# Chunk attention and a Mish feed-forward on one core: transposes behind the output products, one inversion of the sums for two tiles

## The chip, the core and the metric

The kernel runs on one core of a Trainium2 chip. A core has TensorE (products into PSUM), VectorE, ScalarE, GpSimd and SyncE (which here issues the DMAs). Each engine works through its own queue in order and waits at semaphores for the others. The metric is the time of one execution on the device in microseconds (us); a profiled execution also leaves a trace with the start and length of every instruction.

## The reference

Attention within chunks of 64 tokens, for 8 sequences of 576 tokens and 8 heads of 64; then a feed-forward with w_in 512 x 2048 and w_out 2048 x 512 over all 4,608 tokens:

```python
scores = scale * np.matmul(q_c, k_c.transpose(0, 1, 2, 4, 3))
scores = scores - np.max(scores, axis=-1, keepdims=True)
attn = np.exp(scores)
attn = attn / (np.sum(attn, axis=-1, keepdims=True) + 1e-09)
out = np.matmul(attn, v_c)
...
h = x @ w_in
sp = np.where(h > 20.0, h, np.log1p(np.exp(np.minimum(h, 20.0))))
g = h * np.tanh(sp)
return (g @ w_out).astype(np.float32)
```

## The kernel before

**Tiles.** A tile is 128 tokens, two chunks. A *pair* is two tiles (256 tokens), a *block* is two pairs (512 tokens), and there are 9 blocks, 18 pairs. Everything that needs precision goes through TensorE as two fp32r parts, a high one and the rest (`xh`, `xl` for the attention's result, `wi_h`, `wi_l`, `wo_h`, `wo_l` for the weights, `gh`, `gl` for the gate).

**Slots.** The main loop has a slot for each step `s` = 0 to 144, one for each of 16 groups of 128 columns of w_in in each block, and one more to finish. In slot `s` TensorE runs `up(s + 1)`, twelve products of 512 columns into the PSUM tile `h` (of which two exist), and `down(s - 1)`, twelve products into the four accumulators `o`. ScalarE turns `h` into `z` by `mish(s + 1)`; VectorE (in every second step of the first block ScalarE) makes `gh` of it in `g_hi(s)`, and VectorE `gl` in `g_lo(s)`. `down(s - 1)` needs `gh` and `gl` of the slot before.

**The weights.** They come as 64-bit numbers and are taken apart during the first 16 slots, two of them in each slot: ScalarE scales (`w_scale`, two instructions), VectorE puts the bits together (`w_bits`, two), ScalarE rounds to the high part (`w_hi`), VectorE subtracts (`w_lo`). In slot `s` this ends with `wo` of column group `s`, which `down(s)` needs in the next slot, and `wi` of group `s + 3`. The tile between the two engines (`wic`, `woc`, tag `c`) has three buffers: a scaling needs the one that VectorE's subtraction, three weights earlier, gives back.

**The attention of a pair** is spread over seven slots `k0` to `k0 + 6` by `plan`: scores (0), max and subtraction (1), Exp, sum, inversion (2), norm (3), transposes and their copy to SBUF (4), values products (5), the two parts of x (6). `k0` is 1 and 8 in the first block, and 16 more for each block on, so the transposes of the first two steady pairs stand in slots 5 and 12. The scores `s`, the transposes `pt` and the values products `av` all use one PSUM tile, tag `a` (`HOME`), of which there is one: each must have been read out before the next is written. The values products need both the copy `ps` and that tile.

**The order** on each engine is the order in which the code is written (`manual_schedule`), so the calls in `slot` set it. In slot 4 of a pair TensorE has `up`, transposes, `down`; ScalarE has the high part of one weight, in even slots `gh`, two scalings, the copy, `mish`, the high part of the next weight, two scalings.

**The prologue** does pairs 0 and 1 tile by tile (`FIRST`, `SECOND`), the two tiles in different PSUM tiles, with the weights' first steps in between. `keep_busy(n)` puts `n` filler products (two records each in the trace) into TensorE's queue ahead of a wait; they write to a tile nobody reads.

Of the kernel before, what the change touches and what calls it, by code (L numbers as in the profile page):

```python
# [9 lines left out]
F32 = mybir.dt.float32  # L10
# [4 lines left out]
ALU = mybir.AluOpType  # L15
AX = mybir.AxisListType

P = 128
CHUNK = 64
# [4 lines left out]
def kernel(  # L24
# [17 lines left out]
    nc = tc.nc  # L42
# [7 lines left out]
    NG = H // 2  # L50
# [4 lines left out]
    sm_p = ctx.enter_context(tc.tile_pool(name="sm", bufs=2))  # L55
# [74 lines left out]
    def w(step, n):  # L130
        if n < len(order):
            steps[step](*order[n])


    st = {}
    xts = {}
    BOTH = slice(0, 2)
# [44 lines left out]
    def small(j, name, t):  # L182
        n = t.stop - t.start
        o = sm_p.tile([P, 2, n * NG], F32, name=f"{name}_{j}_{t.start}", tag=name)
        st[j][name, t.start] = o
        return o
# [21 lines left out]
    def a_exp(j, t=BOTH):  # L208
        p = st[j]["p"][:, t]
        nc.scalar.activation(out=p, in_=p, func=AF.Exp, scale=SCALE)  # L210

    def a_inverse(j, t=BOTH):
        p = st[j]["p"][:, t].rearrange("p t g c k -> p (t g) c k")
        r = small(j, "r", t)
        nc.vector.tensor_reduce(out=r.rearrange("p c n -> p n c"), in_=p, op=ALU.add, axis=AX.X)  # L215
        nc.vector.tensor_scalar(out=r, in0=r, scalar1=1e-9, scalar2=None, op0=ALU.add)
        nc.vector.reciprocal(out=r, in_=r)

    def a_norm(j, t=BOTH):
        p = st[j]["p"][:, t].rearrange("p t g c k -> p c (t g) k")  # L220
        r = st[j]["r", t.start]
        nc.vector.tensor_tensor(  # L222
            out=p, in0=p, in1=r.unsqueeze(3).broadcast_to([P, 2, r.shape[2], CHUNK]), op=ALU.mult
        )

    def a_transpose(j, ts=BOTH, place=HOME):
        d = st[j]
        d["pt", ts.start] = place[0].tile([P, 2, NG, P], F32, name=f"pt_{j}_{ts.start}", tag=place[1])
        for t in range(ts.start, ts.stop):
            for g in range(NG):  # L230
                nc.tensor.transpose(  # L231
                    out=d["pt", ts.start][:, t - ts.start, g],
                    in_=d["p"][:, t, g].rearrange("p c k -> p (c k)"),
                    identity=ident,
                )

    def a_copy(j, t=BOTH):
        d = st[j]
        if t.start == 0:
            d["ps"] = at.tile([P, 2, H, CHUNK], F32, name=f"ps_{j}", tag="A")  # L240
        nc.scalar.copy(  # L241
            out=d["ps"][:, t].rearrange("p t h k -> p (t h k)"),
            in_=d["pt", t.start][:, : t.stop - t.start].rearrange("p t g n -> p (t g n)"),
        )

    def a_values(j, t=BOTH, place=HOME):
        small_mm(banks(j, "av", t, place), st[j]["v"], st[j]["ps"], t)
# [110 lines left out]
    FIRST, SECOND = slice(0, 1), slice(1, 2)  # L358

    def prologue():  # L360

        A, B = slice(0, PTOK), slice(PTOK, TOK)
        O0, O2 = (ps_o, "o0"), (ps_o, "o2")
        room = xp.tile([P, 2, 2, H, CHUNK], F32, name="room_qk", tag="xh")
        room_v = xp.tile([P, 2, 2, H, CHUNK], F32, name="room_v", tag="xl")
        load_qk(0, None, (FIRST, SECOND), (nc.sync, nc.scalar))
        w("load", 0)
        load_v(0, room_v[:, 0])
        load_qk(1, (room[:, 0], room[:, 1]), (FIRST, SECOND))
        w("load", 1)  # L370
        load_v(1, room_v[:, 1])
        w("load", 2)
        w("load", 3)
        for t, place in (FIRST, HOME), (SECOND, O0):
            keep_busy(7 if t == FIRST else 3)
            a_scores(0, t, place)
            a_max(0, t)
            a_sub(0, t)
            a_exp(0, t)
        w("scale", 0)  # L380
        for t, place in (FIRST, O2), (SECOND, HOME):
            a_inverse(0, t)
            a_norm(0, t)
            keep_busy(9 if t == FIRST else 3)
            a_transpose(0, t, place)
            a_copy(0, t)
        w("bits", 0)
        w("hi", 0)
        w("lo", 0)
        for t, place in (FIRST, O0), (SECOND, O2):  # L390
            a_values(0, t, place)
        for t in FIRST, SECOND:
            a_hi(0, t)
            a_lo(0, t)
        w("scale", 1)
        for t, place in (FIRST, HOME), (SECOND, O0):
            a_scores(1, t, place)
            a_max(1, t)
            a_sub(1, t)
            a_exp(1, t)  # L400
        w("scale", 2)
        w("load", 4)
        up(0, A)
        for t, place in (FIRST, O2), (SECOND, HOME):
            a_inverse(1, t)
            a_norm(1, t)
            keep_busy(8 if t == FIRST else 4)
            a_transpose(1, t, place)
            a_copy(1, t)
        w("bits", 1)  # L410
        w("hi", 1)
        w("bits", 2)
        for t, place in (FIRST, O0), (SECOND, O2):
            a_values(1, t, place)
        for t in FIRST, SECOND:
            a_hi(1, t)
            a_lo(1, t)
        w("hi", 2)
        w("scale", 3)
        w("load", 5)  # L420
        w("lo", 1)
        w("lo", 2)
        w("bits", 3)
        w("scale", 4)
        up(0, B)
        up(1, last="w")
        mish(0)
        load_qk(2)
        w("load", 6)
# [8 lines left out]
    def slot(s):  # L438
        a = plan.get(s, {})
        n = 2 * s + 3  # L440

        if 1 <= s and s + 1 < N:
            up(s + 1, last="w")
        if 4 in a:
            a_transpose(a[4])
        if 5 in a:
            a_values(a[5])
        if 0 in a:
            a_scores(a[0])
        if 1 <= s <= N:  # L450
            down(s - 1)

        w("load", n + 4)
        w("hi", n)
        if s < N:
            g_hi(s)
            g_lo(s)
        w("scale", n + 2)
        w("bits", n + 1)
        w("lo", n)  # L460
        if 1 in a:
            a_max(a[1])
        if 3 in a:
            a_norm(a[3])
        if 4 in a:
            a_copy(a[4])
        if 2 in a:
            a_exp(a[2])

        w("load", n + 5)  # L470
        if 6 in a:
            a_hi(a[6])
        if s + 1 < N:
            mish(s + 1)
        w("hi", n + 1)
        w("scale", n + 3)
        w("bits", n + 2)
        w("lo", n + 1)
        if 1 in a:
            a_sub(a[1])  # L480
        if 2 in a:
            a_inverse(a[2])
        if 6 in a:
            a_lo(a[6])
        if -2 in a and a[-2] > 2:
            load_qk(a[-2])
        if 1 in a:
            load_v(a[1])
        if s >= 1 and s % NF == 0:
            store(s // NF - 1)  # L490
# [43 lines left out]
```

## Time and profile before

| | |
|---|---|
| median of 3 runs | 878.25 us (878.2 to 879.17) |
| the profiled execution | 878.64 us, its span 876.9 us |
| TensorE busy | 860.9 us (98%), 5984 instructions |
| weight loads of TensorE | 709.4 us (81%) |
| VectorE busy | 342.9 us (39%), 534 instructions |
| ScalarE busy | 253.4 us (29%), 360 instructions |
| mean granted clock of TensorE | 0.996 |

The profile has a page with sums over the span, and the trace answers questions on stretches, engines and single instructions. A row of the trace in order of time gives the start in us, the length, the engine, the line of the kernel, the operation, output and inputs, and how many like instructions in a row it stands for; in brackets the idle time of the engine ahead of it and what ended that. L162 is a score or values product, L201 the subtraction of the maximum, L210 Exp, L215 to L217 sum, addition and reciprocal, L222 the norm, L231 a transpose, L241 the copy, L288 `up`, L300 `mish`, L308 and L313 `gh` and `gl` on VectorE, L326 `down`, L356 a filler, L89 and L93 the two scalings, L99 the bits, L114 and L117 the high and the low part of a weight. The products of TensorE overlap: the start of the next is the surer measure, the end of one is modelled. The granted clock is a share of full speed: 1.00 is 2.4 GHz and 0.50 is 1.2 GHz.

### The profile page before, as it was taken

Reading aid. Unit: us, or ns where it says so; the run is one execution under the profiler, and the core shown is the slowest. Engines: PE = TensorE matmul, PEld = TensorE weight load, DVE = VectorE, ACT = ScalarE, POOL = GpSimd, SP = SyncE. Lnnn points to the kernel's source line nnn. Section 1 sums busy time; section 2 is a strip of 40 time slices with the busy share of each in tenths; the row PEclk is TensorE's granted clock in tenths of the full one; section 3 lists DMA queues with packets and bytes.
Section 4 is the critical chain, followed back from the end, with each engine's and each line's share of the span. In section 5 each row is a group of like instructions: output and inputs, shape, how many; then the busy total and the mean of one; then the engine's idle time right before and its main releaser. Section 6 shows DMA issues by size and latency. Waiting matters only on the chain.

```text
span 876.9 us, 13659 instructions
## 1 busy us (share of the span) xinstructions
PE 860.9 (98%) x5984; PEld 709.4 (81%) x5984; DVE 342.9 (39%) x534; ACT 253.4 (29%) x360; POOL 0.7 (0%) x6
## 2 busy tenths in 40 slices
PE   7989999999999999999999999999999999999996
PEld 7778888888888888888888888888888888888885
DVE  6898844242434233323424242423242243322221
ACT  4887832121312122221213131212222131321111
POOL 0000000000000000000000000000000000000000
PEclk9999999999999999999999999999999999999999
DMA  6657612101310120111120121012011201001002
GB/s 265 218 183 227 191 40 58 49 25 49 73 49 25 49 73 25 50 28 53 41 73 4 46 73 49 25 50 73 35 39 49 63 24 59 1 5 44 1 0 49
DMA packets 25180, 55.41 MB, mean 63 GB/s; under 512 B 2592, under 2 KB 2592, under 8 KB 25120
## 3 DMA queue, kind: packets, MB, share of 16 engines
q1 hardware_dynamic: 24832, 54.01, 20.6%
q8 instruction: 47, 0.77, 0.4%
q10 hardware_dynamic: 288, 0.52, 0.2%
q14 instruction: 13, 0.11, 0.0%
HBM read 45.09 MB, written 9.44 MB: 62 GB/s over the span
## 4 chain that ended last, share of the span: by engine, by line
PE 91%; DVE 5%; ACT 3%; issue 1%; DMA 0%; SPq 0%; POOLq 0%; POOL 0%; DVEq 0%; ACTq 0%
PE o L326 43%; PE h L288 41%; PE s L162 2%; PE av L162 2%; PE pt L231 2%; DVE wic L99 1%; DVE woc L99 1%; DVE p L222 1%; PE spare L356 0%; DVE m L189 0%; DVE wo_l L117 0%; ACT L300 0%; DVE r L215 0%; DVE wi_l L117 0%; ACT L210 0%
## 5 line engine op out<-in xcount | busy, mean ns | idle before, releaser
L308 DVE CAST gh<-z 128x512 fp32r<-128x512 f32 x136 | 57.9, 426 | 455.9 <-PE o L326 455.9
L326 PE MATMUL o<-wo_h,gl 128*128 128x512 f32 x576 | 229.6, 399 | 0.0
L326 PE MATMUL o<-wo_l,gh 128*128 128x512 f32 x576 | 225.2, 391 | 0.1
L326 PE MATMUL o<-wo_h,gh 128*128 128x512 f32 x576 | 225.3, 391 | 0.0
L300 ACT ACTIVATE z<-h 128x512 f32<-128x512 f32 x144 | 86.1, 598 | 454.3 <-PE h L288 348.5
L288 PE MATMUL h<-xh,wi_l 128*128 128x512 f32 (+1 forms) x580 | 154.4, 388 | 0.9 <-ACT xh L262 0.9
L288 PE MATMUL h<-xl,wi_h 128*128 128x512 f32 (+1 forms) x580 | 154.2, 388 | 0.3 <-ACT z L300 0.3
L288 PE MATMUL h<-xh,wi_h 128*128 128x512 f32 (+1 forms) x580 | 154.2, 388 | 0.0
L326 PEld LDWEIGHTS o<-wo_h,gl 128*128 128x128 f32 x576 | 108.5, 188 | 23.3
L288 PEld LDWEIGHTS h<-xh,wi_l 128*128 128x128 f32 x580 | 108.4, 188 | 23.4 <-ACT xh L262 1.0
L326 PEld LDWEIGHTS o<-wo_h,gh 128*128 128x128 f32 x576 | 108.5, 188 | 22.8
L288 PEld LDWEIGHTS h<-xl,wi_h 128*128 128x128 f32 x580 | 108.2, 188 | 22.9 <-ACT z L300 0.7
L288 PEld LDWEIGHTS h<-xh,wi_h 128*128 128x128 f32 x580 | 108.4, 188 | 22.3
L326 PEld LDWEIGHTS o<-wo_l,gh 128*128 128x128 f32 x576 | 108.6, 189 | 21.8 <-DVE wo_l L117 0.5
L313 DVE TENSOR_TENSOR gl<-z,gh 128x512 fp32r<-128x512 f32 x144 | 99.6, 692 | 9.5 <-ACT gh L306 4.8
L241 ACT COPY ps<-pt 128x1024 f32<-128x1024 f32 (+1 forms) x20 | 18.6, 928 | 83.4 <-PE pt L231 83.4
L338 DVE COPY ob<-o 128x512 f32<-128x512 f32 x18 | 12.5, 692 | 52.7 <-ACT ob L340 30.9
L300 ACT ACT_TABLE_LOAD x17 | 21.8, 1283 | 34.5 <-PE h L288 34.5
L231 PE MATMUL pt<-ident,p 128*128 128x128 f32 x144 | 19.1, 273 | 5.6 <-DVE p L222 5.6
L189 DVE TENSOR_REDUCE m<-s 128x16 f32<-128x1024 f32 (+1 forms) x20 | 22.2, 1112 | 5.9 <-PE s L162 5.8
L231 PEld LDWEIGHTS pt<-ident,p 128*128 128x128 f32 x144 | 16.4, 139 | 8.8 <-issue 3.5
L162 PEld LDWEIGHTS s<-k,q 64*64 64x64 f32 x1088 | 17.9, 137 | 6.0 <-issue 5.9
(38 smaller groups left out, 384.5 us busy)
## 6 DMA issues: line engine op xcount, KB each, us to landing
out<-ob SPq DMA_DIRECT2D x72, 128.0 KB, 2.4
wis<-in_w_in SPq DMA_DIRECT2D x16, 512.0 KB, 3.6
wos<-in_w_out SPq DMA_DIRECT2D x16, 512.0 KB, 3.9
q<-in_q SPq DMA_DIRECT2D x16, 512.0 KB, 3.7
k<-in_k SPq DMA_DIRECT2D x16, 512.0 KB, 3.7
v<-in_v SPq DMA_DIRECT2D x16, 512.0 KB, 3.9
room_v<-in_v SPq DMA_DIRECT2D x2, 512.0 KB, 7.5
k<-in_k ACTq DMA_DIRECT2D x2, 256.0 KB, 3.9
```

The costliest lines, as they stand in the source:

```text
L99: nc.vector.scalar_tensor_tensor(out=c, in0=x, scalar=mask, in1=d["a"][:, :, 0] if op == ALU.logical_shift_left else c, op0=op, op1=ALU.bi ...
L162: nc.tensor.matmul(o[h * CHUNK : (h + 1) * CHUNK, c, t - ts.start, g], lhsT=l[rows, t, 2 * g + h], rhs=r[rows, t, 2 * g + h], start=True, ...
L189: nc.vector.tensor_reduce(out=small(j, "m", t), in_=st[j]["s", t.start].rearrange("p c t g k -> p c (t g) k"), op=ALU.max, axis=AX.X,)
L222: nc.vector.tensor_tensor(out=p, in0=p, in1=r.unsqueeze(3).broadcast_to([P, 2, r.shape[2], CHUNK]), op=ALU.mult)
L231: nc.tensor.transpose(out=d["pt", ts.start][:, t - ts.start, g], in_=d["p"][:, t, g].rearrange("p c k -> p (c k)"), identity=ident,)
L241: nc.scalar.copy(out=d["ps"][:, t].rearrange("p t h k -> p (t h k)"), in_=d["pt", t.start][:, : t.stop - t.start].rearrange("p t g n -> p ...
L288: nc.tensor.matmul(h[:, cols], lhsT=w_[:, f, kt], rhs=x[:, kt, cols], start=(n == 0), stop=(n == 3 * NK - 1),)
L300: nc.scalar.activation(out=d["z"], in_=d["h"], func=AF.Mish)
L308: nc.vector.tensor_copy(out=d["gh"], in_=d["z"])
L313: nc.vector.tensor_tensor(out=d["gl"], in0=d["z"], in1=d["gh"].bitcast(F32), op=ALU.subtract)
L326: nc.tensor.matmul(acc[t], lhsT=g[:, sl], rhs=w_[:, f], start=(f == 0 and n == 0), stop=(f == NF - 1 and n == 2),)
L338: nc.vector.tensor_copy(out=o, in_=acc[t])
```

## The change

In a slot, a pair's transposes move from between `up` and the output products to behind the output products, and their copy moves from the middle of that slot to the beginning of ScalarE's queue in the next one, ahead of the values products. The sum of a tile (`a_sum`) is separated from the addition and the reciprocal (`a_inverse`), which in the prologue now run once for both tiles of a pair, after both sums; the tile `r` is one for both, in the order tile, head group, chunk, and sum and norm run through `p` in its memory's order. Of the prologue the diff shows pair 0; pair 1 is changed alike.

```diff
-    def a_inverse(j, t=BOTH):
-        p = st[j]["p"][:, t].rearrange("p t g c k -> p (t g) c k")
-        r = small(j, "r", t)
-        nc.vector.tensor_reduce(out=r.rearrange("p c n -> p n c"), in_=p, op=ALU.add, axis=AX.X)
+    def a_sum(j, t=BOTH):
+        d = st[j]
+        if t.start == 0:
+            d["r"] = sm_p.tile([P, 2, 2 * NG], F32, name=f"r_{j}", tag="r")
+        nc.vector.tensor_reduce(
+            out=d["r"][:, t].rearrange("p t n -> p (t n)"),
+            in_=d["p"][:, t].rearrange("p t g c k -> p (t g c) k"),
...
+    def a_inverse(j):
+        r = st[j]["r"]
         nc.vector.tensor_scalar(out=r, in0=r, scalar1=1e-9, scalar2=None, op0=ALU.add)
         nc.vector.reciprocal(out=r, in_=r)
 
     def a_norm(j, t=BOTH):
-        p = st[j]["p"][:, t].rearrange("p t g c k -> p c (t g) k")
-        r = st[j]["r", t.start]
+        p = st[j]["p"][:, t].rearrange("p t g c k -> p (t g c) k")
+        r = st[j]["r"][:, t].rearrange("p t n -> p (t n)")
...
+        for t in FIRST, SECOND:
+            a_sum(0, t)
+        a_inverse(0)
         w("scale", 0)
         for t, place in (FIRST, O2), (SECOND, HOME):
-            a_inverse(0, t)
             a_norm(0, t)
             keep_busy(9 if t == FIRST else 3)
             a_transpose(0, t, place)
...
-        if 4 in a:
-            a_transpose(a[4])
         if 5 in a:
+            a_copy(a[5])
             a_values(a[5])
         if 0 in a:
             a_scores(a[0])
         if 1 <= s <= N:
             down(s - 1)
+        if 4 in a:
+            a_transpose(a[4])
...
-        if 4 in a:
-            a_copy(a[4])
...
         if 2 in a:
+            a_sum(a[2])
             a_inverse(a[2])
```

TensorE in slot 5 of the main loop (`h` is `up`, `o` is `down`, `pt` the transposes of pair 2), before:

```order
L288 MATMUL h_706<-xl_246,wi_h 128x512 x4
L288 MATMUL h_706<-xh_245,wi_h 128x512 x4
L288 MATMUL h_706<-xh_245,wi_l 128x512 x4
L231 MATMUL pt_0_719<-ident,p_598 128x128 x8
L326 MATMUL o_0_509<-wo_h,gl_686 128x512
L326 MATMUL o_0_509<-wo_l,gh_684 128x512
L326 MATMUL o_0_509<-wo_h,gh_684 128x512
```

And now, at the end of slot 5 and the beginning of slot 6:

```order
L335 MATMUL o_2_510<-wo_h,gl_680 128x512
L335 MATMUL o_2_510<-wo_l,gh_678 128x512
L335 MATMUL o_2_510<-wo_h,gh_678 128x512
L240 MATMUL pt_0_725<-ident,p_592 128x128 x8
L297 MATMUL h_758<-xl_243,wi_h 128x512 x4
L297 MATMUL h_758<-xh_242,wi_h 128x512 x4
L297 MATMUL h_758<-xh_242,wi_l 128x512 x4
```

The twelve output products, which stood behind the transposes, now stand ahead of them.

ScalarE in slots 5 and 6 (`ps` is the copy, `z` the gate activation, `wi_h` and `wo_h` the high parts of weights, `wic`, `wis` and `woc`, `wos` the scalings), before:

```order
L93 ACTIVATE wos_681<-wos_681 128x512
L241 COPY ps_753<-pt_0_719 128x1024
L300 ACTIVATE z_757<-h_706 128x512
L114 CAST wi_h<-wic_700 128x512
L89 ACTIVATE wic_760<-wis_695 128x512
L93 ACTIVATE wis_695<-wis_695 128x512
L114 CAST wo_h<-woc_747 128x512
L306 CAST gh_827<-z_757 128x512
```

And now:

```order
L93 ACTIVATE wos_681<-wos_681 128x512
L309 ACTIVATE z_749<-h_700 128x512
L114 CAST wi_h<-wic_694 128x512
L89 ACTIVATE wic_752<-wis_689 128x512
L93 ACTIVATE wis_689<-wis_689 128x512
L250 COPY ps_771<-pt_0_725 128x1024
L114 CAST wo_h<-woc_741 128x512
L315 CAST gh_821<-z_749 128x512
```

The copy moved behind the gate activation, a cast and two scalings; the two casts behind it are the first work of slot 6.

VectorE in the prologue, pair 0, from the second tile's maximum on (`m` maximum, `p` probabilities, `r` sums), before:

```order
L189 TENSOR_REDUCE m_1_165<-s_1_148 128x8
L201 TENSOR_TENSOR p_142<-s_1_148,m_1_165 128x2x4x64
L215 TENSOR_REDUCE r_0_172<-p_142 128x4x2
L216 TENSOR_SCALAR r_0_172<-r_0_172 128x8
L217 RECIPROCAL r_0_172<-r_0_172 128x8
L222 TENSOR_TENSOR p_142<-p_142,r_0_172 128x2x4x64
L215 TENSOR_REDUCE r_1_193<-p_142 128x4x2
L216 TENSOR_SCALAR r_1_193<-r_1_193 128x8
L217 RECIPROCAL r_1_193<-r_1_193 128x8
L222 TENSOR_TENSOR p_142<-p_142,r_1_193 128x2x4x64
```

And now:

```order
L189 TENSOR_REDUCE m_1_165<-s_1_148 128x8
L201 TENSOR_TENSOR p_142<-s_1_148,m_1_165 128x2x4x64
L216 TENSOR_REDUCE r_169<-p_142 128x8 x2
L225 TENSOR_SCALAR r_169<-r_169 128x16
L226 RECIPROCAL r_169<-r_169 128x16
L231 TENSOR_TENSOR p_142<-p_142,r_169 128x512 x2
```

Both sums now stand ahead of the first norm, and one addition and one reciprocal are gone. TensorE's order in the prologue, fillers included, is as before.

## Rows read from the trace of the kernel before

**Rows 1.** The page: an engine's busy time, and VectorE's largest group with its wait

```profile
PE 860.9 (98%) x5984; PEld 709.4 (81%) x5984; DVE 342.9 (39%) x534; ACT 253.4 (29%) x360; POOL 0.7 (0%) x6
...
L308 DVE CAST gh<-z 128x512 fp32r<-128x512 f32 x136 | 57.9, 426 | 455.9 <-PE o L326 455.9
```

**Rows 2.** Stretches: length, busy us of PE, PEld, DVE, ACT, POOL, clock, DMA

```profile
40.00:60.00 20.00, 17.45 (x81) 14.00 (x80) 18.46 (x28) 16.77 (x26) 0.00 (x0) 1.00 0.61 204
```

**Rows 3.** TensorE in order of time, slots 5 and 6

```profile
55.49 1.07 PE L288 MATMUL h<-xh,wi_l 128*128 128x512 f32 x4
59.03 1.06 PE L231 MATMUL pt<-ident,p 128*128 128x128 f32 x8 [2.46 <-DVE p L222]
...
67.11 1.16 PE L162 MATMUL av<-ps,v 64*64 64x64 f32 x64
```

**Rows 4.** Stretches in the prologue and in slot 5 (the clock is third from last)

```profile
11.00:12.00 1.00, 0.94 (x9) 0.75 (x7) 0.90 (x4) 0.58 (x1) 0.00 (x0) 1.00 0.93 365
...
60.50:61.00 0.50, 0.50 (x3) 0.38 (x2) 0.50 (x2) 0.50 (x2) 0.00 (x0) 0.50 0.00 0
```

**Rows 5.** Chain that ended last, merged: start, us, what; slot 5, then later slots

```profile
60.09 4.34 PE o L326 x12
...
152.66 2.72 PE h L288 x12
155.38 0.87 PE pt L231 x8
```

**Rows 6.** VectorE in order of time, slots 4 and 5, then slot 9

```profile
57.06 0.68 DVE L117 TENSOR_TENSOR wo_l<-woc,wo_h 128x512 fp32r<-128x512 f32 x1
57.67 1.22 DVE L222 TENSOR_TENSOR p<-p,r 128x1024 f32<-128x1024 f32 x1
...
63.12 0.69 DVE L117 TENSOR_TENSOR wo_l<-woc,wo_h 128x512 fp32r<-128x512 f32 x1
...
83.46 0.43 DVE L308 CAST gh<-z 128x512 fp32r<-128x512 f32 x1 [1.50 <-PE o L326]
```

**Rows 7.** ScalarE in order of time, slot 5

```profile
62.03 0.99 ACT L241 COPY ps<-pt 128x1024 f32<-128x1024 f32 x1
...
64.50 0.68 ACT L93 ACTIVATE wis<-wis 128x512 int32<-128x512 uint32 x1
```

**Rows 8.** All engines in order of time, slots 12 and 13

```profile
102.68 1.06 PE L231 MATMUL pt<-ident,p 128*128 128x128 f32 x8 [0.22 <-DVE p L222]
...
106.40 0.69 DVE L99 SCALAR_TENSOR_TENSOR wic<-wis,wic 128x512 uint32<-128x512 uint32 x1
...
107.47 0.61 ACT L114 CAST wi_h<-wic 128x512 fp32r<-128x512 f32 x1
...
109.11 0.61 ACT L114 CAST wo_h<-woc 128x512 fp32r<-128x512 f32 x1
...
109.15 1.16 PE L162 MATMUL av<-ps,v 64*64 64x64 f32 x64
```

**Rows 9.** All engines in order of time, the prologue's pair 0

```profile
8.77 0.63 ACT L210 ACTIVATE p<-p 128x512 f32<-128x512 f32 x1 [0.85 <-DVE p L201]
...
9.81 0.69 DVE L222 TENSOR_TENSOR p<-p,r 128x512 f32<-128x512 f32 x1
...
10.64 0.63 PE L231 MATMUL pt<-ident,p 128*128 128x128 f32 x4 [1.19 <-DVE p L222]
...
11.11 0.83 PE L356 MATMUL spare<-ident 128*128 128x128 f32 x6
...
12.41 0.63 PE L231 MATMUL pt<-ident,p 128*128 128x128 f32 x4 [0.47 <-DVE p L222]
```

**Rows 10.** Groups by form: busy us, mean ns of one, idle time before

```profile
L215 DVE TENSOR_REDUCE r<-p 128x8 f32<-128x512 f32 x4 | 2.7, 680 | 0.0
...
L217 DVE RECIPROCAL r<-r 128x16 f32<-128x16 f32 x16 | 4.1, 254 | 0.6
L216 DVE TENSOR_SCALAR r<-r 128x16 f32<-128x16 f32 x16 | 2.8, 175 | 0.5
```

More of the change, by code (lines that the diff above doesn't have):

```diff
@@ L210, in a_exp @@
         nc.scalar.activation(out=p, in_=p, func=AF.Exp, scale=SCALE)
-    def a_inverse(j, t=BOTH):
-        p = st[j]["p"][:, t].rearrange("p t g c k -> p (t g) c k")
-        r = small(j, "r", t)
-        nc.vector.tensor_reduce(out=r.rearrange("p c n -> p n c"), in_=p, op=ALU.add, axis=AX.X)
+    def a_sum(j, t=BOTH):
[5 more added lines that the diff above has]
+            in_=d["p"][:, t].rearrange("p t g c k -> p (t g c) k"),
+            op=ALU.add,
+            axis=AX.X,
+        )
+    def a_inverse(j):
+        r = st[j]["r"]
         nc.vector.tensor_scalar(out=r, in0=r, scalar1=1e-9, scalar2=None, op0=ALU.add)
@@ L219, in a_norm @@
     def a_norm(j, t=BOTH):
-        p = st[j]["p"][:, t].rearrange("p t g c k -> p c (t g) k")
-        r = st[j]["r", t.start]
+        p = st[j]["p"][:, t].rearrange("p t g c k -> p (t g c) k")
+        r = st[j]["r"][:, t].rearrange("p t n -> p (t n)")
         nc.vector.tensor_tensor(
-            out=p, in0=p, in1=r.unsqueeze(3).broadcast_to([P, 2, r.shape[2], CHUNK]), op=ALU.mult
+            out=p, in0=p, in1=r.unsqueeze(2).broadcast_to([P, r.shape[1], CHUNK]), op=ALU.mult
         )
@@ L400, in prologue @@
             a_exp(1, t)
+        for t in FIRST, SECOND:
+            a_sum(1, t)
+        a_inverse(1)
         w("scale", 2)
@@ L404, in prologue @@
         for t, place in (FIRST, O2), (SECOND, HOME):
-            a_inverse(1, t)
             a_norm(1, t)
```

## The prediction

> **What bounds the kernel now.** I read the page's busy shares first, then the stretches, then the order of time on single engines. TensorE is busy 98% of the span, and the largest group of VectorE has waited 455.9 us for TensorE's output products [rows 1]. So nearly everywhere TensorE is the bound, and moving work on the other two engines buys nothing there. The exception is the start: between 40 and 60 us TensorE is busy 17.45 of 20 us, VectorE 18.46 and ScalarE 16.77 [rows 2]. There the two engines split the weights into two parts, and TensorE runs into them. The largest hole is in slot 5, at the first steady pair's transposes: the last four products of `up` start at 55.49, one product takes 2.72 / 12 = 0.227 us [rows 3, 5], so what follows could start at 56.40; the transposes start at 59.03, because `p` is normalised from 57.67 to 58.89 [rows 3, 6]. A second cost follows: after TensorE stood 2.46 us, the granted clock is 0.50 at 60.5 us, that is 1.2 instead of 2.4 GHz [rows 3, 4], and the twelve output products there take 4.34 us against 2.72 for twelve elsewhere, 1.6 us more [rows 5]. What the change does to this stretch, to the same place of the next pair (slots 12 and 13) and to the prologue decides the time.
>
> **The slots in which TensorE is the bound (14 of 16 pairs).** Eight transposes cost 0.87 us between two blocks of products [rows 5]; moved from behind `up` to behind `down` they are as many, between the same two kinds of neighbours. The copy now starts when they end, while the next `up` (2.72 us) runs; it takes 0.99 [rows 7], so 1.7 us of cover is left before the values products need it. Without that cover each pair would pay up to 0.99. I take 0. No row shows transposes between `down` and `up`; the nearest others are the prologue's, four in 11.11 - 10.64 = 0.47 [rows 9], 0.94 for eight, 0.07 more than here. So I bound the move by 0.07 a pair either way, 1.0 us in all, for the range. The sum and the norm run through as many elements in another order, on an engine that waits: 0.
>
> **Slots 5 and 6 (the first steady pair).** All times here are on the clock of the profile before. In slot 5 the output products now stand right behind `up`. The first can start at 56.40. The second reads `wo_l`, which VectorE writes from 57.06 for 0.68 us [rows 6], so a new wait of about 1.2 us takes the place of the old one: the second starts near 57.8, the remaining eleven end near 60.4, the transposes (whose `p` is ready at 58.89) near 61.3, and `up` of slot 6 near 64.0. Up to here 3 us are won against before, where the values products started at 67.11 [rows 3].
> But these need the copy. In ScalarE's queue it now stands behind the rest of slot 5 (the gate activation, a cast, two scalings) and not ahead of them. The first of these scalings needs a buffer that VectorE gives back when it ends the row of 63.12, at 63.81 [rows 6]; so the two cannot move up, and the second stays at 64.50 [rows 7]. The copy follows near 65.1 and ends near 66.1. The values products start at 66.1 instead of 64.1, a wait of 2.0 us, and **the gain left is 67.1 - 66.1 = 1.0 us**. Queued behind the copy are the cast of `wo_h` and the cast of `gh`, for which VectorE's `gl` waits: VectorE comes up to 0.8 us late in slot 6. At 83.46 it stood 1.50 us waiting for TensorE [rows 6], which is where its delay and TensorE's lead meet; from there on all engines run about 1.0 us earlier.
>
> **Slots 12 and 13 (the second pair).** Before, the transposes waited 0.22 us by the row [rows 8], some 0.4 against the pitch; the move saves that. But the copy again moves behind the rest of its slot. The cast that stood at 107.47 needs bits that VectorE ends at 106.40 + 0.69 = 107.09, so it can start at 107.1. From that cast to the next slot's first ScalarE instruction it was 109.11 - 107.47 = 1.64 us [rows 8]. With the copy in that place it starts near 108.8, ends near 109.8, and the values products follow at 109.9 instead of 109.15 [rows 8]: **0.8 us lost**, the saved 0.4 included. The bounds: a gain of 0.4, if ScalarE were free in time, and a loss of 1.0, the whole copy.
>
> **The prologue (two pairs, where VectorE is on the path).** Before, the first tile's sum, addition, reciprocal and norm ran while the second tile was still in Exp. Now the second sum stands ahead of the first norm. Exp of the second tile ends at 8.77 + 0.63 = 9.40 [rows 9]; then come the sum 0.680, the addition 0.175, the reciprocal 0.254 [rows 10] with four hand-overs of some 0.04: the first norm starts near 10.65 instead of 9.81. One addition and one reciprocal fewer bring the second norm's end some 0.3 us forward. But on TensorE the fillers (`keep_busy`) stand between the two tiles' transposes. Before, the first transposes started 0.83 after their norm, at 10.64, the fillers at 11.11, and the second tile's transposes at 12.41, when their norm was there [rows 9]. Now the first start at 11.48, the fillers (six records, 0.11 from start to start as for the transposes) at 11.95, and the second tile's cannot start before 12.6: 0.2 late, although their norm is ready near 12.0. The second pair repeats the pattern with eight records: 0.84 + 0.47 + 0.88 = 2.19 against 12.41 - 10.64 = 1.77, 0.4 late. Of these 0.6 ScalarE's weight cast, which stands ahead of the next step, hides some 0.1: **0.5 us lost**, with 0.2 and 0.6 as bounds. Without the fillers it would be a gain of 0.3 a pair.
>
> **The sum.** -1.0 + 0.8 + 0.5 = +0.3 us. The profiled execution took 878.64 (876.9 of span and 1.74 around it), so 878.9; the median of the runs is 0.39 below that execution, hence **878.6**.
>
> **A rule weighed.** A wait of TensorE of 1.19 us left the granted clock at 1.00 [rows 4, 9], that of 2.46 us did not [rows 3, 4]; the new ones of 2.0 us lie between. [...]
>
> **The rivals.**
> *The clock falls again* (slower). Place: the 2.0 us wait ahead of the values products in slot 6. Price: 1.6 [rows 5]. It decides from where, between 1.19 and 2.46 us, a wait drops the clock. 878.6 + 1.6 = 880.2. For it: 2.0 is nearer to 2.46. Against: the transposes, which before came right after the wait, now stand 2.7 us of products ahead of it.
> *The clock falls in the prologue* (slower). The idle time ahead of the first tile's transposes grows from 1.19 to 2.0 us [rows 9]. The work behind it is smaller than in slot 5; I price it at 1.0 to 1.6: 879.6 to 880.2.
> *The copy does not hold TensorE* (faster). If ScalarE reached it by 63.0, 3.0 us would be won in slot 6 and 0.4 in slot 13: -3.4 + 0.5 = -2.9, so 878.25 - 2.9 = 875.4. Against it stands the scaling at 64.50, held by VectorE and not by TensorE [rows 6, 7].
> *The move costs or saves in every pair*: 1.0 us either way, 877.6 or 879.6, inside the forecast's own range.
>
> **How the numbers follow.** The forecast, two losses that eat the gain, with its terms' bounds (877.2 to 879.8): 0.58. The clock in slot 6: 0.20; in the prologue: 0.10. The copy that does not hold: 0.12. The range from 876.4 to 881.0 leaves out the copy's rival and some 0.04 above, where the clock falls twice. A measurement of this kernel can tell about 0.2% from no change, 1.76 us: faster is below 876.5, slower above 880.0. Faster: the copy's 0.12, and 0.04 from the forecast's edge, 0.16. Slower: the clock's 0.30, less 0.08 that end just under 880.0, and 0.02 from the forecast's edge, 0.24. Within: 0.60.
>
> **What would show each step.** In slot 5 no wait for the norm, a wait of about 1.2 us after the first output product, ended by `wo_l`, and the granted clock at 1.00 through 60 us. In slot 6 a wait of about 2.0 us ahead of the values products, released by ScalarE's copy, and about 1.2 in slot 13. In the prologue the first tile's transposes some 0.85 late, the second's 0.2 and 0.4, with the fillers right ahead of them. From 130 us on, slots as long as before. I am wrong if the values products of slot 6 follow `up` without a wait, if the clock shows 0.50 before the last output product, or if a late slot with transposes takes another time than 2.72 + 0.87 + 2.72.

## The result, and the profile after

The kernel after takes 880.12 us (median of 16 executions), the kernel before, measured beside it, 878.33 (16): a ratio of 1.0021, 95% interval 1.0014 to 1.0029. It is slower by about 1.8 us. The prediction said 878.6 in a range of 876.4 to 881.0. The range holds the result, but the likeliest case does not: 880.12 is where the clock's rivals stood (880.2; 879.6 to 880.2). The profiled execution of after took 881.87 us, 880.1 of it span, with 876.9 of span before.

The line numbers of after are others than those of before: L231 is now the norm, L240 a transpose, L250 the copy, L271 and L274 the high part and the rest of x, L297 `up`, L309 `mish`, L317 `gh`, L335 `down`, L365 a filler. Runs built on before (e1, e7) keep before's numbers, where L265 is the rest of x; in b1 all lines behind the inserted ones are three later.

The page, TensorE's row and VectorE's largest group, to be read beside [rows 1]: the averages show nothing. TensorE is 98% busy in both, and VectorE still waits for the output products.

```profile
PE 861.7 (98%) x5984; PEld 710.5 (81%) x5984; DVE 342.3 (39%) x530; ACT 254.9 (29%) x360; POOL 0.7 (0%) x6
...
L317 DVE CAST gh<-z 128x512 fp32r<-128x512 f32 x136 | 57.9, 426 | 456.5 <-PE o L335 456.5
```

So the difference has to be looked for place by place. **The prologue**, kernel after, VectorE's norms (one row for both tiles) and TensorE in order of time; it answers to [rows 9]:

```profile
10.62 1.29 DVE L231 TENSOR_TENSOR p<-p,r 128x512 f32<-128x512 f32 x2
```

```profile
11.46 1.09 PE L240 MATMUL pt<-ident,p 128*128 128x128 f32 x4 [2.03 <-DVE p L231]
12.34 1.49 PE L365 MATMUL spare<-ident 128*128 128x128 f32 x6
13.63 1.06 PE L240 MATMUL pt<-ident,p 128*128 128x128 f32 x4
```

and the stretches there (length, busy us of PE, PEld, DVE, ACT, POOL, granted clock, DMA share, GB/s):

```profile
11.00:12.00 1.00, 0.54 (x3) 0.57 (x4) 1.00 (x3) 0.00 (x0) 0.00 (x0) 0.73 1.00 383
12.00:13.00 1.00, 1.00 (x7) 1.00 (x6) 0.96 (x2) 0.41 (x1) 0.00 (x0) 0.50 1.07 406
13.00:14.00 1.00, 1.00 (x6) 1.00 (x6) 0.24 (x1) 0.17 (x1) 0.00 (x0) 0.50 1.03 403
14.00:15.00 1.00, 1.00 (x21) 0.67 (x22) 0.00 (x0) 0.28 (x1) 0.00 (x0) 0.57 1.05 414
```

The norm stands at 10.62 and the transposes at 11.46, within 0.03 of the forecast. But after TensorE stood 2.03 us the clock is at 0.50 (1.2 GHz) until shortly before 15 us. The six fillers take 1.49 instead of 0.83 us, and since they stand ahead of the second tile's transposes, these come at 13.63 instead of 12.6.

**Slots 5 and 6**, kernel after, VectorE's low part of `wo`, then TensorE in order of time, then ScalarE around the copy, then the stretches behind (as [rows 3, 4, 6, 7]):

```profile
58.94 0.68 DVE L117 TENSOR_TENSOR wo_l<-woc,wo_h 128x512 fp32r<-128x512 f32 x1
```

```profile
59.77 0.47 PE L335 MATMUL o<-wo_l,gh 128*128 128x512 f32 x1 [1.10 <-ACT wi_h L114]
...
62.37 1.03 PE L240 MATMUL pt<-ident,p 128*128 128x128 f32 x8
63.16 1.17 PE L297 MATMUL h<-xl,wi_h 128*128 128x512 f32 x4
...
67.91 1.16 PE L162 MATMUL av<-ps,v 64*64 64x64 f32 x64 [1.77 <-ACT ps L250]
```

```profile
66.30 0.66 ACT L93 ACTIVATE wis<-wis 128x512 int32<-128x512 uint32 x1
66.87 0.98 ACT L250 COPY ps<-pt 128x1024 f32<-128x1024 f32 x1
```

```profile
68.00:69.00 1.00, 1.00 (x65) 0.93 (x65) 0.07 (x1) 1.00 (x3) 0.00 (x0) 1.00 0.82 86
69.00:70.00 1.00, 1.00 (x9) 0.82 (x4) 1.00 (x2) 1.00 (x3) 0.00 (x0) 0.74 0.77 311
70.00:71.00 1.00, 1.00 (x4) 0.75 (x3) 0.97 (x3) 0.53 (x3) 0.00 (x0) 0.50 0.39 148
71.00:72.00 1.00, 1.00 (x4) 0.81 (x3) 1.00 (x2) 0.96 (x2) 0.00 (x0) 0.50 0.00 0
72.00:73.00 1.00, 1.00 (x4) 0.78 (x4) 0.97 (x3) 1.00 (x3) 0.00 (x0) 0.55 0.47 160
```

The queues do what was forecast: 1.10 us ahead of the second output product, no wait at the transposes, the copy behind the second scaling, 1.77 us ahead of the values products. For the first of these waits the trace names ScalarE's cast of `wi_h`, which that product does not read; it reads `wo_l`, which VectorE ends at 59.62, 0.15 ahead of it. Then the clock falls here too, which it did in slot 5 before. **Slots 12 and 13**, TensorE (as [rows 8]):

```profile
107.42 1.03 PE L240 MATMUL pt<-ident,p 128*128 128x128 f32 x8
...
112.38 1.16 PE L162 MATMUL av<-ps,v 64*64 64x64 f32 x64 [1.20 <-ACT ps L250]
```

Where the two profiles come apart, in `up` of slot 5 and `up` behind the values products, first before, then after:

```profile
53.68 1.07 PE L288 MATMUL h<-xl,wi_h 128*128 128x512 f32 x4
71.06 1.07 PE L288 MATMUL h<-xl,wi_h 128*128 128x512 f32 x4
```

```profile
55.56 1.07 PE L297 MATMUL h<-xl,wi_h 128*128 128x512 f32 x4
73.45 1.07 PE L297 MATMUL h<-xl,wi_h 128*128 128x512 f32 x4
```

From the start of the same work before and after: the `up` of slot 5 is 1.88 late (55.56 against 53.68), the values products of slot 6 are 0.80 late (67.91 against 67.11 in [rows 3]), the next `up` behind them 2.39 (73.45 against 71.06), the values products of slot 13 3.23 (112.38 against 109.15 in [rows 8]), and `up` at 121.77 still 3.24 (118.53 before). The span as a whole is 3.2 longer. So nothing is added in the other 14 pairs, and all of it is in three places.

### The profile page after: what moved, and what is told of

It reads as the page before. It is cut to its first block, busy times and chain, and to the rows that moved or that the text cites. A ratio compares the mean times of both kernels' runs of the same rounds, so it can differ in the third digit from the quotient of the medians.

```text
span 880.1 us, 13658 instructions
## 1 busy us (share of the span) xinstructions
PE 861.7 (98%) x5984; PEld 710.5 (81%) x5984; DVE 342.3 (39%) x530; ACT 254.9 (29%) x360; POOL 0.7 (0%) x6
## 4 chain that ended last, share of the span: by engine, by line
PE 89%; DVE 5%; ACT 3%; issue 1%; DMA 1%; SPq 0%; DVEq 0%; ACTq 0%
PE o L335 43%; PE h L297 41%; PE s L162 2%; PE av L162 2%; PE pt L240 2%; DVE woc L99 1%; DVE wic L99 1%; DVE wo_l L117 1%; DVE m L189 0%; DMA k<-in_k 0%; ACT L309 0%; DVE p L231 0%; DVE wi_l L117 0%; PE spare L365 0%; ACT ps L250 0%
## 5 line engine op out<-in xcount | busy, mean ns | idle before, releaser
L317 DVE CAST gh<-z 128x512 fp32r<-128x512 f32 x136 | 57.9, 426 | 456.5 <-PE o L335 456.5
L335 PE MATMUL o<-wo_h,gl 128*128 128x512 f32 x576 | 228.3, 396 | 0.0
L309 ACT ACTIVATE z<-h 128x512 f32<-128x512 f32 x144 | 85.9, 596 | 491.1 <-PE h L297 441.4
L335 PE MATMUL o<-wo_l,gh 128*128 128x512 f32 x576 | 225.2, 391 | 1.2 <-ACT wi_h L114 1.1
L335 PE MATMUL o<-wo_h,gh 128*128 128x512 f32 x576 | 225.3, 391 | 0.0
L297 PE MATMUL h<-xl,wi_h 128*128 128x512 f32 (+1 forms) x580 | 155.7, 390 | 0.2 <-ACT z L309 0.2
L297 PE MATMUL h<-xh,wi_l 128*128 128x512 f32 (+1 forms) x580 | 154.3, 388 | 0.8 <-ACT xh L271 0.8
L297 PE MATMUL h<-xh,wi_h 128*128 128x512 f32 (+1 forms) x580 | 154.2, 388 | 0.0
L335 PEld LDWEIGHTS o<-wo_h,gl 128*128 128x128 f32 x576 | 108.5, 188 | 23.9
L335 PEld LDWEIGHTS o<-wo_l,gh 128*128 128x128 f32 x576 | 108.6, 189 | 23.7 <-ACT wi_h L114 1.5
L297 PEld LDWEIGHTS h<-xh,wi_l 128*128 128x128 f32 x580 | 108.4, 188 | 23.3 <-ACT xh L271 0.9
L335 PEld LDWEIGHTS o<-wo_h,gh 128*128 128x128 f32 x576 | 108.4, 188 | 22.8
L297 PEld LDWEIGHTS h<-xh,wi_h 128*128 128x128 f32 x580 | 108.4, 188 | 22.4
L297 PEld LDWEIGHTS h<-xl,wi_h 128*128 128x128 f32 x580 | 107.1, 188 | 21.7 <-ACT z L309 0.7
L250 ACT COPY ps<-pt 128x1024 f32<-128x1024 f32 (+1 forms) x20 | 18.6, 929 | 47.4 <-PE pt L240 47.4
L240 PE MATMUL pt<-ident,p 128*128 128x128 f32 x144 | 19.9, 281 | 3.9 <-DVE p L231 3.9
L162 PEld LDWEIGHTS av<-ps,v 64*64 64x64 f32 x1024 | 16.4, 134 | 8.7 <-issue 4.9
```

The lines of the kernel that those rows point to most:

```text
L162: nc.tensor.matmul(o[h * CHUNK : (h + 1) * CHUNK, c, t - ts.start, g], lhsT=l[rows, t, 2 * g + h], rhs=r[rows, t, 2 * g + h], start=True, ...
L240: nc.tensor.transpose(out=d["pt", ts.start][:, t - ts.start, g], in_=d["p"][:, t, g].rearrange("p c k -> p (c k)"), identity=ident,)
L250: nc.scalar.copy(out=d["ps"][:, t].rearrange("p t h k -> p (t h k)"), in_=d["pt", t.start][:, : t.stop - t.start].rearrange("p t g n -> p ...
L297: nc.tensor.matmul(h[:, cols], lhsT=w_[:, f, kt], rhs=x[:, kt, cols], start=(n == 0), stop=(n == 3 * NK - 1),)
L309: nc.scalar.activation(out=d["z"], in_=d["h"], func=AF.Mish)
L317: nc.vector.tensor_copy(out=d["gh"], in_=d["z"])
```

## The experiments

Two readings are needed to compare them. Each was timed beside the kernel before, whose median was 878.33 in the first four, 878.65 in the next four and 878.59 in the last three. And in the profiled executions the second tile's score products in the prologue start at 6.08 to 7.54 us, in before and after alike and not by any edit (last section). I therefore give, beside the median, the **rest of the span** from those products on; for before that is 876.9 - 6.56 = 870.34, for after 880.1 - 6.53 = 873.57.

| kernel | median, us | all executions | rest of the span, us | clock at 0.50 while TensorE worked, in the profile |
|---|---|---|---|---|
| before (beside after) | 878.33 | 877.28 to 880.48 | 870.34 | slot 5 |
| b1_fill5 | 877.08 | 876.43 to 878.67 | 868.65 | nowhere |
| after | 880.12 | 879.56 to 882.92 | 873.57 | prologue, slot 6 |
| a3_fill_all | 879.01 | 878.42 to 879.67 | 870.52 | nowhere |
| e3_fill | 878.98 | 878.61 to 880.97 | 870.53 | nowhere |
| e1_slot | 879.15 | 878.00 to 881.88 | 870.10 | nowhere |
| e2_prologue | 878.35 | 878.07 to 880.11 | 870.50 | prologue |
| e6_nofill | 878.02 | 877.33 to 879.26 | 869.36 | nowhere |
| e4_copy | 877.32 | 877.08 to 878.80 | 869.17 | prologue |
| e5_values | 877.97 | 876.80 to 879.91 | 868.72 | nowhere |
| e7_slot_copy | 876.18 | 875.68 to 877.94 | 867.68 | nowhere |
| e8_both | 875.59 | 875.38 to 876.94 | 867.01 | nowhere |
| e9_early_lo | 875.77 | 875.37 to 876.40 | 867.53 | nowhere |

Behind TensorE's last product the clock goes to 0.50 in every one of these profiles, where it holds nothing up: in before from 872.6 us, with the last product at 869.5. The mean granted clock of an execution holds this tail too, so it does not tell whether the clock fell in the work: e7 has 0.997 and no such fall, e2 has 0.997 and one.

### The two halves of the change

The slots alone (e1), with the prologue of before:

```diff
-        if 4 in a:
-            a_transpose(a[4])
         if 5 in a:
+            a_copy(a[5])
             a_values(a[5])
...
             down(s - 1)
+        if 4 in a:
+            a_transpose(a[4])
...
-        if 4 in a:
-            a_copy(a[4])
```

> Only the slot part of the change (transposes behind the output products, copy in the next slot); the prologue is the one of before. Theory Q (ScalarE's queue and the clock): -1.0 us in slots 5 and 6 and +0.8 in slots 12 and 13, so -0.2 against before where the clock holds, and +1.4 where it falls after the wait ahead of slot 6's values products; a median between the two. The trace shows that wait at 1.8 to 2.0 us, one of 1.2 in slot 13, and the prologue as before. Rival P (the move costs something in each of the 16 pairs): +1.4 or more with every late slot with transposes longer. Rival S (all of the loss is the late first norm in the prologue): no more than 0.2 from before in every execution.

The prologue alone (e2), with the slots of before; the sums' rows in another order and the one inversion stay:

```diff
+        for t in FIRST, SECOND:
+            a_sum(0, t)
+        a_inverse(0)
...
-            a_inverse(0, t)
             a_norm(0, t)
```

> Only the prologue part (both sums ahead of one inversion); the slots are those of before. Theory Q: +0.6 us where the clock holds and up to +2.0 where it falls behind the 2.0 us that TensorE stands before the first tile's transposes; slot 5 keeps its old wait for the norm of 2.4 us. Rival P: 0. Rival S: the whole +1.8.

e1 came out at 1.0012 of before (1.0003 to 1.0022), e2 at 1.0009 (1.0000 to 1.0018). Neither half is a gain. TensorE in slots 5 and 6 of e1:

```profile
57.84 0.47 PE L326 MATMUL o<-wo_l,gh 128*128 128x512 f32 x1 [1.10 <-ACT wi_h L114]
60.46 1.03 PE L231 MATMUL pt<-ident,p 128*128 128x128 f32 x8
65.99 1.16 PE L162 MATMUL av<-ps,v 64*64 64x64 f32 x64 [1.77 <-ACT ps L241]
```

The same waits as in after, and here the clock stayed at 1.00 behind them. e2 has the counterpart: the wait in slot 5 is as in before, 2.47 us, and this time the clock behind it did not fall:

```profile
60.33 1.06 PE L240 MATMUL pt<-ident,p 128*128 128x128 f32 x8 [2.47 <-DVE p L231]
```

```profile
61.00:62.00 1.00, 1.00 (x8) 0.87 (x7) 1.00 (x2) 0.45 (x1) 0.00 (x0) 1.00 0.39 156
62.00:63.00 1.00, 1.00 (x6) 0.83 (x5) 0.97 (x3) 1.00 (x3) 0.00 (x0) 1.00 0.23 20
```

So the same wait of the same length drops the clock in one execution and not in another. The times hint at it too: e2's eleven lie at 878.07 to 878.35 (six) and at 879.78 to 880.11 (five), with nothing between. None of the upper five was profiled, so that slot 5's fall parts the groups is not shown. This made the loss of slot 5, which I had read from one profile of before, a matter of chance. It had to be measured by itself.

### What the clock is worth in each kernel

In before, ten fillers in slot 5 alone, in the tile that the transposes overwrite:

```diff
         d["pt", ts.start] = place[0].tile([P, 2, NG, P], F32, name=f"pt_{j}_{ts.start}", tag=place[1])
+        if j == PAIRS:
+            for _ in range(10):
+                nc.tensor.matmul(d["pt", 0][:, 0, 0], lhsT=ident, rhs=ident, start=True, stop=True)
```

> The kernel before, with ten filler products in slot 5 ahead of the first steady pair's transposes, written into the transposes' own tile, so that TensorE works while it stood 2.46 us. Nothing else is changed; the fillers (10 x 0.22 = 2.2 us) end before the norm does. Theory C (the clock is what differs between executions of the kernel before: with the fall in slot 5 about 878.3 to 878.7, without it about 877.1): the granted clock stays at 1.00 through 55 to 65 us, the median is 877.1 and nearly no execution is above 877.8. Theory N (the spread has another source, and the fall costs nothing that lasts): the median stays at 878.3.

TensorE in slot 5 of b1, and the stretches:

```profile
56.02 2.39 PE L231 MATMUL pt<-ident 128*128 128x128 f32 x20
58.55 1.09 PE L234 MATMUL pt<-ident,p 128*128 128x128 f32 x8
```

```profile
58.00:60.00 2.00, 1.85 (x15) 1.58 (x14) 1.97 (x4) 0.83 (x3) 0.00 (x0) 1.00 0.61 238
60.00:62.00 2.00, 2.00 (x10) 1.64 (x9) 1.97 (x4) 2.00 (x4) 0.00 (x0) 1.00 0.38 115
```

The transposes come 52.40 us after the second score products, against 59.03 - 6.56 = 52.47 before: the fillers bring them no earlier. Only the clock is different, and the median is 877.08 against 878.65, ratio 0.9982 (0.9972 to 0.9991); the rest of the span is 1.69 shorter. One execution in ten still took 878.67.

In after, first the prologue's holes (e3), then that of slot 6 as well (a3, with products that add zero to an accumulator):

```diff
-            keep_busy(9 if t == FIRST else 3)
+            keep_busy(13 if t == FIRST else 3)
...
-            keep_busy(8 if t == FIRST else 4)
+            keep_busy(11 if t == FIRST else 4)
```

> The changed kernel with four more fillers ahead of the first tile's transposes of pair 0 and three more of pair 1, in time that TensorE stands idle. Theory Q: no wait above 1.4 us in the prologue, the granted clock at 1.00 until slot 6, and the executions that lost up to 1.4 us there win it: 0 to -1.4 against the changed kernel, -0.7 in the median, so +1.1 against before. Rival P and a theory in which the clock in the prologue is hidden: as the changed kernel, +1.8 against before.

```diff
+        spare["zero"] = const.tile([P, P], F32R, name="zero")
+        nc.gpsimd.tensor_tensor(out=spare["zero"], in0=ident, in1=ident, op=ALU.subtract)
...
         if 5 in a:
+            if s == 6:
+                for _ in range(7):
+                    nc.tensor.matmul(acc[0], lhsT=spare["zero"], rhs=wo_h[:, 0], start=False, stop=False)
             a_copy(a[5])
```

> The kernel after with fillers in every hole that it opens: four and three more ahead of the first tile's transposes in the prologue, and seven products that add zero to an accumulator ahead of slot 6's values products, where TensorE waited 1.77 us for the copy. Theory C: no fall in any execution, median 878.8 (span 877.1 and 1.74 around it), and the cluster of executions at 880.4 to 881.0 that the kernel with the prologue's fillers alone still had (3 of 11) is gone. Against the kernel before with its own hole filled, then, 1.7 slower: that is what the change costs without the clock, since its gain in slot 5 was for the most part the clock's. Theory N: 879 to 880, and the upper cluster stays.

TensorE in the prologue of e3, and its stretches there and in slot 6:

```profile
11.50 0.63 PE L240 MATMUL pt<-ident,p 128*128 128x128 f32 x4 [1.14 <-DVE p L231]
11.96 0.83 PE L365 MATMUL spare<-ident 128*128 128x128 f32 x6
12.63 0.60 PE L240 MATMUL pt<-ident,p 128*128 128x128 f32 x4
```

```profile
11.00:15.00 4.00, 3.45 (x110) 3.10 (x110) 2.84 (x5) 2.32 (x5) 0.00 (x0) 1.00 1.03 399
67.00:69.00 2.00, 2.00 (x50) 1.71 (x43) 1.48 (x3) 2.00 (x4) 0.00 (x0) 1.00 0.76 238
69.00:72.00 3.00, 3.00 (x14) 2.46 (x14) 2.97 (x6) 2.47 (x5) 0.00 (x0) 1.00 0.42 119
```

The first tile's transposes start no earlier than in after (11.50), the second tile's 1.0 earlier (12.63, as forecast). The median falls by 1.14, to 878.98, and the rest of the span is 3.04 shorter than after's, since in this execution slot 6 kept its clock as well. Three of e3's eleven executions were still at 880.4 to 881.0; with slot 6 filled too none of a3's eleven is above 879.67. a3's median stays at 879.01, as it would if the middle execution of e3 had no fall in slot 6 either. That the upper three had one is not shown, since only one execution of each kernel was profiled.

Without the clock, then, after against before is a3 against b1: 879.01 - 877.08 = 1.9 us in the medians, 870.52 - 868.65 = 1.87 in the rest of the span. e1 - b1 gives 1.45 of it to the slots, e3 - e1 0.43 to the prologue. The parts add up to after itself: 868.65 + 1.87, a fall in the prologue (1.0 to 1.5, worked out below) and one in slot 6 (1.59) make 873.1 to 873.6, and after has 873.57.

### The queue terms one by one

The fillers between the two tiles, moved ahead of the first (e6):

```diff
-            keep_busy(9 if t == FIRST else 3)
+            keep_busy(13 if t == FIRST else 0)
...
-            keep_busy(8 if t == FIRST else 4)
+            keep_busy(11 if t == FIRST else 0)
```

> The kernel after with the prologue's fillers between the two tiles' transposes moved ahead of the first tile's (13 and 0 in place of 9 and 3; 11 and 0 in place of 8 and 4). Theory Q (the fillers hold the second tile's transposes, 0.2 and 0.4 us, which without them would come 0.3 a pair early; the clock does not fall there any more): 1.1 to 1.2 us under the kernel with the added fillers, so a median of 877.8 and, where slot 6's wait drops the clock, 879.4. Theory V (VectorE's later first norm is the loss, whatever the fillers do): 878.9, as the kernel with the added fillers.

The rest of the span is 1.17 under e3's and the median 0.96. The loss of the prologue was not VectorE's later first norm but the fillers that held the second tile's transposes; without them the one inversion is a gain of 0.43 - 1.17 = -0.74 against the prologue of before.

The copy back in the transposes' own slot, behind the gate activation: with the prologue of after (e4), and with that of before (e7).

```diff
         if 5 in a:
-            a_copy(a[5])
             a_values(a[5])
...
             mish(s + 1)
+        if 4 in a:
+            a_copy(a[4])
```

> The changed kernel with the copy in the same slot as the transposes, right behind the gate activation and ahead of the cast and the two scalings. Theory Q: the transposes end before ScalarE is there, so the waits of 1.8 and 1.2 us ahead of the values products go: -3.0 us against the changed kernel, -3.0 to -4.6 with the clock's fall behind the first of them: 1.2 to 2.8 faster than before. Rival P: as the changed kernel. A rival in which the weights' casts behind the copy then come late and TensorE waits for them instead: the 3.0 us come back as waits for a weight in slots 6 to 8.

> The prologue of before; in the slots the transposes behind the output products, but the copy not in the next slot: it stands in the transposes' own slot, right behind the gate activation. Theory Q (the copy's place in ScalarE's queue holds TensorE in slots 6 and 13, 1.8 and 1.2 us): the values products follow the scores' up without a wait, span 873.4 without a fall of the clock, so 875.1 to 875.4, 3 us under the kernel before; no hole over 1.2 us from slot 5 on. Theory P (the transposes behind the output products cost some hundredths in each of the 16 pairs): 876 or more. Theory D (the place of the copy trades its wait for one at the scores' q and k, 0.6 us in slot 8): 875.7.

e4 came out 2.8 under after (ratio to before 0.9992, 0.9983 to 1.0001), e7 at 0.9972 (0.9961 to 0.9983). TensorE in e4:

```profile
65.22 1.16 PE L162 MATMUL av<-ps,v 64*64 64x64 f32 x64
78.10 1.11 PE L162 MATMUL s<-k,q 64*64 64x64 f32 x61 [0.61 <-PE h L297]
```

The wait in slot 6 is gone; what took its place is a wait in slot 8, ahead of the next pair's scores, 0.61 in e4 and 0.59 in e7. By the rest of the span e7 is 2.42 under e1: 1.77 + 1.20 for the two waits, less 0.59. I had expected 875.1 to 875.4 and, with a wait in slot 8, 875.7; it is 876.18, and the first of these leaves the new wait out. Why 875.7, which counts it, is still 0.5 too low is not shown. The releaser that the trace names for that wait cannot be right, since `up` had ended 0.59 before. VectorE in e7, ahead of these scores at 77.35:

```profile
76.03 1.22 DVE L265 TENSOR_TENSOR xl<-av,xh 128x1024 fp32r<-128x1024 f32 x1
```

It ends at 77.25, and it reads the values from the one PSUM tile into which the scores go. The test is to move it. Both good parts together (e8: e6's prologue, e4's slots), and in e9 also `xl` earlier in VectorE's queue:

```diff
         w("hi", n + 1)
         w("scale", n + 3)
+        if 6 in a:
+            a_lo(a[6])
         w("bits", n + 2)
...
-        if 6 in a:
-            a_lo(a[6])
```

> Slots with the copy behind the gate activation, and the prologue of after with its fillers ahead of the first tile's transposes (13 and 0, 11 and 0). By the earlier runs this prologue is worth 0.7 us against that of before (it came out 1.1 under the kernel with the added fillers, which had lost 0.4). Theory T (TensorE is still what decides up to slot 8): 0.7 under the kernel with the slots alone, 875.5. Theory X (in slot 8 the scores wait for VectorE's xl, which frees their PSUM tile and does not come earlier when TensorE does): their wait grows from 0.6 to some 1.2 us and the time stays at 876.1.

> As the kernel with both parts, and VectorE's xl (the subtraction that gives the PSUM tile back) stands two groups earlier in its slot, ahead of the bits and the low part of a weight that nobody needs before the next slot. Theory X: the scores of slot 8 no longer wait, 0.6 to 1.2 us under the kernel with both parts, 874.9. Theory Z (the bits that now stand behind xl come 1.2 us late for ScalarE's cast of wo, and the next output products wait for that): as much is lost there, no gain.

e8 takes 875.59 (0.9970 of before, 0.9959 to 0.9982): 0.59 under e7, as theory T had it, with the wait in slot 8 unchanged at 0.59. In e9 that wait is gone, which settles who caused it. TensorE in e9:

```profile
75.79 1.16 PE L162 MATMUL s<-k,q 64*64 64x64 f32 x64
...
99.41 0.50 PE L335 MATMUL o<-wo_l,gh 128*128 128x512 f32 x1 [0.24 <-DVE wo_l L117]
...
115.60 1.20 PE L297 MATMUL h<-xl,wi_h 128*128 128x512 f32 x4 [0.31 <-DVE xl L274]
```

But nothing is won (875.77, five executions). Counted from the second score products, the scores of slot 8 start 0.65 ahead of e8's; at the wait for `wo_l` 0.5 of this is lost and at that for `xl` 0.6 (the waits themselves are 0.55 together, and the first products behind them start further apart), and the rest of the span is 0.5 longer than e8's. VectorE reaches that `wo_l` at 98.67 us, in e8 at 98.09: what is taken out in one slot is paid in others, as theory Z had it, though in later slots than it named.

Last, the copy where the change puts it, and the values products moved behind the output products (e5):

```diff
         if 5 in a:
             a_copy(a[5])
-            a_values(a[5])
...
             a_transpose(a[4])
+        if 5 in a:
+            a_values(a[5])
```

> The kernel after, with the copy at the place that the change gave it and the values products moved too, behind the output products of their slot: the copy has 2.7 us of products beside it. Theory Q: the waits of 1.8 us in slot 6 and 1.2 us in slot 13 go, and with the first of them the clock's fall there; the prologue stays with its fall. 880.1 - 3.0 and, where the clock fell, 1.6 more: 876.7 to 877.2, as the kernel with the copy behind the gate activation (877.3). Theory P (the late values make the parts of x late, and the scores behind them wait): 878 or more.

It is 877.97, above what I expected. TensorE in e5:

```profile
12.21 0.63 PE L240 MATMUL pt<-ident,p 128*128 128x128 f32 x4 [2.03 <-DVE p L231]
...
68.04 1.16 PE L162 MATMUL av<-ps,v 64*64 64x64 f32 x64
78.85 1.16 PE L162 MATMUL s<-k,q 64*64 64x64 f32 x64 [1.26 <-DVE xl L274]
```

Both waits for the copy are gone, but later values make later parts of x, and the scores of slot 8 wait 1.26 us (theory P's mechanism). By the rest of the span, 3.0 won less 1.3 given back is 1.7; e3, which has no fall either, lies 1.81 above. And the 2.03 us wait in the prologue did not drop the clock in this execution, though it had in after, e2 and e4.

## Why the prediction was right or wrong

The range holds the result, but by the room that it left for the clock's rivals and not by the forecast.

**Slots with TensorE as the bound: right.** The lead of 3.24 at 121.8 us is still 3.2 at the end; the rival of 0.07 a pair is out.

**Slots 5 and 6: right as a sum against that profile.** Forecast: waits of 1.2 and 2.0, values products 1.0 earlier. Measured: 1.10 and 1.77, and 1.88 - 0.80 = 1.08 won from the `up` of slot 5 to the values products.

**Slots 12 and 13: right.** Forecast 0.8 lost and a wait of 1.2; measured 3.23 - 2.39 = 0.84 and 1.20.

**The prologue's queue: right.** Forecast 0.5 lost, by the fillers; measured 0.43 (e3 - e1), and e6 shows the fillers as the cause.

**The sum of the queues: right.** Forecast +0.3 against the profiled execution of before; after without any fall of the clock has 870.53 (e3) or 870.52 (a3), before's profile 870.34: +0.2.

**The clock: the step that failed.** The sum takes the profiled execution of before, with its fall in slot 5, as the kernel, and an after without a fall as the likeliest. Two things were wrong in it. First, the gain of 1.0 in slots 5 and 6 is the clock's: a fall costs 1.7 (before against b1). Without it slots 5 and 6 lose 0.6 to 0.7, and with the 0.8 of slots 12 and 13 the slots' part loses 1.45 (e1 against b1). Second, the waits that the change makes are of the length at which the clock may fall. The prologue's 2.03 dropped it in three profiles of four (after, e2, e4), at a price of 1.0 to 1.5: the start of slot 5's transposes, counted from the second score products, is 62.37 - 6.53 = 55.84 in after and 61.52 - 6.13 = 55.39 in e4, against 60.92 - 6.57 = 54.35 in e3. (In e5, which has after's own prologue and no fall, it is 61.62 - 7.28 = 54.34: up to there e3's added fillers change nothing but the clock.) Slot 6's 1.77 dropped it in after's profile, 1.59 more, and not in those of e1, e3 and e6. I gave the two places 0.20 and 0.10, gave both together some 0.04, and took slot 6 for the likelier; it was the prologue that carried the median (after less e3: 1.14). Thirteen of after's sixteen executions lie above 879.67, the highest of a3, so an execution without a fall was most likely the exception, and the two falls together, as in the profile, took it out of the range (881.87). The argument that I set against the fall in slot 6, that the transposes no longer stand right behind the wait, did not hold: the clock fell there in after.

That the median of 880.12 is so near to the 880.2 of the rival in slot 6 is luck: that time has slot 6's fall in it, and it is the prologue's that the median holds (1.14, after less e3).

The Trainium skill ("TensorE: Matmul & The Clock Gate", section "Loop structure matters more than you think") counts a long wait for DMA between matmuls as what makes TensorE go cold. No run here has such a wait; here waits of 1.77 to 2.47 us for VectorE's norm and ScalarE's copy were followed by the fall in some executions and not in others.

**The rival that the copy does not hold TensorE** did not come true, and e4 and e7 show what it would have been worth: where ScalarE reaches the copy in time, the two waits' 2.97 us less the 0.59 that slot 8 takes back, 2.42 measured (e7 against e1).

## What to carry to other kernels

Before a stall's price is read from one profile, see whether it holds a fall of the clock, and fill the stall with idle products once: the difference is what removing the stall is really worth, and here that turned the slots' gain of 1.08 less 0.84, some 0.2, into a loss of 1.45. When a block is moved on one engine, look where its follow-up lands in the next engine's in-order queue (here the copy behind two scalings) and place that by hand too; the version that did, with the fillers ahead of the first wait and not between the tiles, takes 875.59 us and beats both kernels. A wait removed at the head of a chain is worth only what the next engine's queue leaves: 0.6 of e7's gain went to `xl`, and moving `xl` only moved the wait.

## What the runs showed of the hardware that I had not expected

Whether a wait drops the granted clock is not settled by its length alone. Waits of 1.10 to 1.26 us were followed by 1.00 in every profile; those of 1.77, 2.03 and 2.46 to 2.47 us by 0.50 in some executions and by 1.00 in others, in the same place and behind the same work. What decides it I could not see, and no experiment here was made on it. The prologue's second pair has a wait of 1.82 to 1.84 us in after, e4 and e5, between 1.77 and 2.03 in length, and the clock stayed at 1.00 behind it in all three; three profiles do not tell its place from chance. In after:

```profile
23.15 0.63 PE L240 MATMUL pt<-ident,p 128*128 128x128 f32 x4 [1.84 <-DVE p L231]
```

The fall does not come with the wait but can follow when TensorE is already at work: in after's slot 6 it resumed at 67.91, the stretch from 68 to 69 us has not yet fallen, and that from 69 to 70 shows 0.74. With it, fillers that are meant to bridge a wait become the obstacle themselves: six took 1.49 us instead of 0.83 with the next transposes behind them.

The start of the second score products wandered by 1.46 us (6.08 to 7.54) between profiled executions, as much as most of the effects here; spans had to be counted from there. It is for the most part not the first transfers: the first score products start at 4.59 to 4.64 us in eleven of the thirteen profiles (5.00 in e6 and 5.04 in after, where the trace names the DMA of `k`). What differs is how long the same work takes: the first score products 0.69 to 1.13 us, the six fillers behind them 0.94 to 1.65. That is the order of the 1.49 for six fillers at 0.50 in after's prologue, but the granted clock reads 1.00 from 0 to 8 us in every profile, so what slows them is not shown.
